# The layers behind attention in an order written by hand: the first stage goes on in cycles, the second runs in two parts of four and five chunks

## The chip, the core and the metric

The kernel runs on one core of a Trainium2 chip. The metric is the device time of one execution in microseconds (us), as the median of several runs. Four engines compute, each with a queue of its own that it works off in order: TensorE (PE, matmuls into PSUM; PEld is its weight load), VectorE (DVE), ScalarE (ACT) and GpSimd (POOL). SyncE (SP) issues the DMAs. [...]

## What is computed

Masked attention over 8 batches, 8 heads, 576 positions and 64 dimensions, and behind it a two-layer network over the 4608 tokens:

```
scores = scale * q @ k^T                 # 8 x 8 x 576 x 576
thresh = max(scores) - tau               # per row
scores = where(scores >= thresh, scores, -1e9)
attn   = softmax(scores);  x = (attn @ v) as 4608 tokens x 512
h = x @ w_in                             # w_in 512 x 2048, float64
g = max(h, 0) + alpha * min(h, 0)        # alpha per column of h
out = g @ w_out                          # w_out 2048 x 512, float64
```

The weights come as float64. Each matrix is used as the sum of a high and a low part in a float32 matmul format, and each product is three matmuls: high x high, low x high and high x low.

## The kernel before

The 2048 hidden columns are 16 chunks of 128. Chunks 0 to 6 (`fcs1`) are the first stage: it runs beside attention, for 18 groups of 256 tokens (`groups1`). Chunks 7 to 15 (`fcs2`) are the second stage, for 9 groups of 512 tokens, behind it. The first stage leaves its sums in DRAM (`part`); the second adds its own and writes `out`.

**One group, one chunk.** The first layer (`layer1_into`, L188 to L201) is 12 matmuls: four slices of the 512 inputs, three products each, with `xh` and `xl`, the parts of x, as the moving operand. Then comes the prelu on DVE, a copy to the high part on ACT and a subtraction for the low part on POOL (`split_g`, L213). The second layer (`layer2`, L220) is three matmuls of 512 columns for each block of 128 tokens and chunk: high part with `woh`, high part with `wol`, low part with `woh`. A group of 256 tokens has two such blocks, a group of 512 has four.

**Decode.** `Split64` (L102) turns a 128 x 512 piece of float64 words into two parts: a DMA of 512 KB (`load`), two ACT passes (`size`, L123 and L124), five or six DVE passes (`clamp` L127, `shift` L130, `sign` L135, `power` L140, `rest` L148 and, on DVE or POOL, L149), an ACT copy (`round`, L144) and a POOL sum (`join`, L152).

**Order.** Everything up to the end of attention stands in a block with an order written by hand for PE, ACT, DVE and POOL (L791): each engine takes its instructions in the order of the text. SP isn't one of these engines. The text is a loop over cycles (L804); a cycle is one of nine steps of a pair of heads, 288 in all (`total`), and `at_cycle(i, fn)` puts a step into cycle i. `Mlp.cycle` (L713) fills each cycle with work of the first stage up to a length of `CYCLE` = 2.6: at most one first-layer chunk (counted as 1.31) and second-layer matmuls (0.216 each). `step_l1` (L664) loads x, splits it one cycle later and holds the next group's chunks back by three cycles (`gap`); a chunk's prelu falls one cycle and its split two cycles after its matmuls, and the group's second layer starts three cycles after its last chunk. `ps_m` has four PSUM buffers for chunks and accumulators alike; in the first stage's pool x, its parts and the block `po` that goes to DRAM have one buffer each.

Behind the loop the order isn't written by hand: a scheduler orders the queues. `Mlp.drain` (L728) does the groups that are left, with four of the second stage's 18 weight pieces after each (`decode_some`, L853; their words have two buffers, tag `w0`), then come the pieces that are left, and then the second stage (L888 to L904): for each group of 512 tokens x in one piece, nine chunks through `hidden` (L868), and four blocks of 27 matmuls each into `accb`, whose result is added on DVE to the sums read back into `pin` (L903) and stored.

In the trace `pha` and `phb` are the first-layer sums of the first and second stage, `acca` and `accb` those of the second layer, `ga` and `gb` the parts behind the prelu, `xr` a piece of x as loaded, `wri`/`wro` the raw words and `wti`/`wto` the working tiles of a piece of `w_in` or `w_out`.

## Time and profile before

| | us |
|---|---|
| median of three runs | 1400.59 (1400.41 to 1401.59) |
| span of the profiled execution | 1397.3 |
| last matmul of attention starts | 830.5 |
| first matmul of the second stage's first group (`phb`) | 941.5 |
| first matmul into `accb` | 969.1 |
| last matmul into `accb` starts | 1393.1 |
| PE busy in 800 to 900 and in 900 to 1000 | 93.3 and 92.0 |
| DVE busy in 800 to 900 and in 900 to 1000 | 74.9 and 67.8 |
| one `xl` split on POOL, 1024 elements a partition | 2.40 (median) |

The span is that of one profiled execution, from its first to its last instruction. "Busy" is the time in which an engine has an instruction under way; matmuls overlap, so the duration of one (0.39 us for 512 columns) is longer than the distance from one to the next. A row of a group of instructions gives the line, the engine, the operation, output <- inputs, the shapes and the count, then busy time and the mean length of one in ns, and the engine's idle time ahead of them with what ended it. A row of the timeline gives start and length in us, and in brackets the idle time before it. A row of the chain of waits gives start and length of one link of the chain that ended last.

### The profile page before, as it was taken

What the parts mean: (1) busy time and instruction counts of PE and PEld (TensorE: products, weight loads), DVE (VectorE), ACT (ScalarE), POOL (GpSimd) and SP (SyncE); (2) the same over time, 40 slices, a digit from 0 to 9 for tenths busy, and PEclk for the clock granted to TensorE, in tenths of its full rate; (3) what the DMA queues carried; (4) which work ended last, traced back from release to release, by engine and by line L of the source; (5) the groups of instructions that cost most, each with busy time, mean ns of one, the idle gap of its engine ahead of it and who ended that gap; (6) DMA issues with size and microseconds to landing.
All of it is one profiled execution on the core that took longest, in us unless ns stands there. A gap on an engine that the chain in (4) does not pass through costs nothing.

```text
span 1397.3 us, 23301 instructions
## 1 busy us (share of the span) xinstructions
PE 1339.4 (96%) x8116; PEld 1181.2 (85%) x8116; DVE 975.7 (70%) x1933; ACT 820.9 (59%) x1843; POOL 762.3 (55%) x821
## 2 busy tenths in 40 slices
PE   5888899999999999999999999888999999999998
PEld 4556789999999999999999998777888888888887
DVE  6999988888888898898888957986323323323332
ACT  7788888888888888888888854453112012111100
POOL 3776676666676666576676557566434124223311
PEclk9999999999999999999999999999999999999999
DMA  8643634545545444454454214433320220111011
GB/s 249 184 127 106 180 105 122 162 116 142 147 117 150 139 134 131 132 154 127 128 160 132 83 57 153 132 109 128 121 74 17 91 91 33 59 61 42 19 61 38
DMA packets 94628, 157.67 MB, mean 113 GB/s; under 512 B 14160, under 2 KB 39024, under 8 KB 94512
## 3 DMA queue, kind: packets, MB, share of 16 engines
q1 hardware_dynamic: 94512, 156.19, 38.4%
q8 instruction: 65, 1.06, 0.3%
q14 instruction: 51, 0.42, 0.1%
HBM read 85.53 MB, written 28.46 MB: 82 GB/s over the span
## 4 chain that ended last, share of the span: by engine, by line
PE 80%; DVE 9%; ACT 4%; DMA 2%; issue 2%; POOL 2%; SPq 0%; DVEq 0%; POOLq 0%; ACTq 0%
PE phb L194 16%; PE accb L224 16%; PE s L395 10%; PE av L542 10%; PE acca L224 9%; PE pha L194 9%; PE t L439 7%; DVE p L430 2%; DVE nmx L410 2%; DMA wri<-in_moe_w_in_dram 1%; PE tk L455 1%; DVE wti L135 1%; POOL wi L152 1%; ACT xb L555 1%; ACT xa L553 1%
## 5 line engine op out<-in xcount | busy, mean ns | idle before, releaser
L410 DVE TENSOR_REDUCE nmx<-s 128x1 f32<-128x576 f32 x288 | 217.0, 753 | 72.6 <-PE s L395 69.5
L215 ACT ACTIVATE gb<-ptb 128x512 fp32r<-128x512 f32 x81 | 50.9, 630 | 337.7 <-DVE ptb L873 337.3
L218 POOL TENSOR_TENSOR gb<-ptb,gb 128x512 fp32r<-128x512 f32 x81 | 104.4, 1290 | 257.0 <-ACT gb L215 256.8
L224 PE MATMUL acca<-wo,ga 128*128 128x512 f32 x756 | 230.7, 419 | 7.2 <-ACT ga L215 4.0
L224 PE MATMUL accb<-wo,gb 128*128 128x512 f32 x972 | 221.9, 389 | 0.0
L224 PEld LDWEIGHTS accb<-wo,gb 128*128 128x128 f32 x972 | 182.4, 188 | 37.9
L430 DVE SCALAR_TENSOR_TENSOR p<-s,thr,p 128x576 f32<-128x576 f32 x256 | 206.6, 807 | 1.3 <-ACT thr L423 0.9
L194 PE MATMUL phb<-xh,wi 128*128 128x512 f32 x648 | 202.9, 392 | 1.1 <-ACT xh L180 1.1
L194 PE MATMUL pha<-xh,wi 128*128 128x256 f32 x1008 | 199.7, 284 | 3.7 <-DVE pta L873 3.4
L418 ACT ACTIVATE p<-s,nmx 128x576 f32<-128x576 f32 x256 | 190.0, 742 | 10.8 <-DVE nmx L410 10.5
L395 PE MATMUL s<-kh,qst 128*128 128x288 f32 x640 | 142.2, 312 | 38.1 <-DVE p L430 23.3
L194 PEld LDWEIGHTS pha<-xh,wi 128*128 128x128 f32 x1008 | 163.8, 190 | 9.9 <-DVE pta L873 4.6
L224 PEld LDWEIGHTS acca<-wo,ga 128*128 128x128 f32 x756 | 132.8, 191 | 28.6 <-ACT ga L215 5.3
L439 PE MATMUL t<-ident,p 128*128 128x128 f32 x1024 | 154.6, 274 | 0.0
L395 PEld LDWEIGHTS s<-kh,qst 128*128 128x128 f32 x640 | 101.4, 193 | 61.5 <-issue 29.4
L903 DVE TENSOR_TENSOR ob<-accb,pin 128x512 f32<-128x512 f32 x36 | 24.2, 689 | 181.9 <-PE accb L224 181.9
L194 PEld LDWEIGHTS phb<-xh,wi 128*128 128x128 f32 x648 | 122.6, 189 | 27.2 <-ACT xh L180 1.5
L194 PE MATMUL pha<-xl,wi 128*128 128x256 f32 x504 | 142.2, 282 | 0.0
L872 DVE TENSOR_SCALAR ptb<-phb,alpha_sb 128x512 f32<-128x512 f32 x81 | 60.7, 751 | 108.5 <-PE phb L194 96.4
L395 PE MATMUL s<-kl,qst 128*128 128x288 f32 x640 | 133.8, 299 | 0.0
L194 PE MATMUL phb<-xl,wi 128*128 128x512 f32 x324 | 127.2, 393 | 3.6 <-POOL xl L182 3.6
L439 PEld LDWEIGHTS t<-ident,p 128*128 128x128 f32 x1024 | 126.5, 141 | 0.1
(117 smaller groups left out, 2772.6 us busy)
## 6 DMA issues: line engine op xcount, KB each, us to landing
kr<-in_k_dram SPq DMA_DIRECT2D x31, 320.0 KB
rb<-rvd SPq DMA_DIRECT2D x64, 144.0 KB
xs<-xa SPq DMA_DIRECT2D x32, 288.0 KB
part<-po SPq DMA_DIRECT2D x36, 256.0 KB
pin<-part SPq DMA_DIRECT2D x36, 256.0 KB
out_dram<-ob SPq DMA_DIRECT2D x36, 256.0 KB
vr<-in_v_dram SPq DMA_DIRECT2D x28, 320.0 KB
qr<-in_q_dram SPq DMA_DIRECT2D x31, 288.0 KB
```

What stands on the lines that cost most here:

```text
L194: nc.tensor.matmul(ph[:, :n], w[:, c, :], xx[:, c, :n], start=(c == 0 and ti == 0), stop=(c == NCC - 1 and ti == 2),)
L215: nc.scalar.activation(g[:, 0, :n], t[:, :n], AF.Copy)
L218: nc.gpsimd.tensor_tensor(g[:, 1, :n], t[:, :n], f(g[:, 0, :n]), op=ALU.subtract)
L224: nc.tensor.matmul(acc[:m, :], gg[:, g, o : o + m], w, start=(first and ti == 0), stop=(last and ti == 2))
L395: nc.tensor.matmul(ps[:, h, :288], w, kk[:, a + h * 288 : a + (h + 1) * 288], start=(ki == 0 and i == 0), stop=(ki == 1 and i == n - 1),)
L410: nc.vector.tensor_reduce(self.nmx[:, j : j + 1], self.S[u][0][:, :, :288], axis=AX.XY, op=ALU.max, negate=True)
L418: nc.scalar.activation(pj, ps[:, :, :288], AF.Exp, bias=nmx[:, j : j + 1], scale=1.0)
L430: nc.vector.scalar_tensor_tensor(pj, ps[:, :, :288], thr[:, j : j + 1], pj, op0=ALU.is_ge, op1=ALU.mult, accum_out=self.sm[:, c : c + 1])
L439: nc.tensor.transpose(tb[:, c, :], pt[:, j, j * D + c * P : j * D + (c + 1) * P], ident)
L542: nc.tensor.matmul(pa[:m, :n], w, x, start=(part == 0 and c == 0), stop=(part == z.parts[-1] and c == NKC))
L872: nc.vector.tensor_scalar(t[:, :n], ph[:, :n], 0.0, alpha_sb[:, fc : fc + 1], op0=ALU.min, op1=ALU.mult)
L903: nc.vector.tensor_tensor(ob[:m], acc[:m], pi_[:m], op=ALU.add)
```

## The change

The written order now holds to the end of the program, and the drain and the scheduler's second stage are gone.

- The cycle loop goes on past `total` until the first stage is empty. There `used` is 0, so a cycle holds 2.6 of the first stage's work alone; a chunk taken at or after `total` (`alone`) has its prelu in two DVE passes (`prelu`) instead of one on DVE, one on ACT and one on POOL, and its high part on ACT.
- At cycle `total + CLOSE` (297) attention's memory is given up. From there the eight pieces of the second stage's first part (chunks 7 to 10) are decoded step by step, one piece every 2.5 cycles (`DEC2` = 5), with three buffers for the raw words, and x of its first group is loaded and split by slices (`fetch_x`, 512 columns a slice, two `xr` buffers).
- The second stage runs in two parts: chunks 7 to 10 over all nine groups of 512 tokens, then chunks 11 to 15 over all nine again. A cycle there is one first-layer chunk or one block of the second layer. Part one adds its sums to those in `part` and stores them there again; part two adds its own and stores to `out`. The ten pieces of part two are decoded under part one, one every six cycles (`DEC3` = 6). x is fetched for the next group in each group, so twice in all.

```diff
-TAIL = 4
+CLOSE = 9
+DEC2, DEC3 = 5, 6
...
+    def prelu(pool, gn, fc, n, ph, name, bufs):
+        t = pool.tile([P, gn], F32, tag="pt", name=f"pt{name}", bufs=bufs)
+        nc.vector.tensor_scalar(t[:, :n], ph[:, :n], 0.0, alpha_sb[:, fc : fc + 1], op0=ALU.min, op1=ALU.mult)
+        nc.vector.scalar_tensor_tensor(t[:, :n], ph[:, :n], 0.0, t[:, :n], op0=ALU.max, op1=ALU.add)
+        return t
...
+            alone = i >= total
+
             def act(ph=ph):
+                if alone:
+                    st[fi] = (prelu(mem.mp1, G1, fcs1[fi], n, ph, name, 2),)
+                    return
                 st[fi] = prelu1(mem.mp1, G1, fcs1[fi], n, ph, name, 2)
                 prelu2(*st[fi], n)
...
+    def decode_at(c, pool, w, fc, io, load):
+        if load is not None:
+            at_cycle(load, w.load)
         at_cycle(c, w.size)
         at_cycle(c + 1, w.clamp)
         at_cycle(c + 2, w.shift)
         at_cycle(c + 3, w.sign)
         at_cycle(c + 4, w.power)
+        at_cycle(c + 4, lambda: w.round(weight(pool, fc, io)[:, 0]))
         at_cycle(c + 5, w.rest)
+        at_cycle(c + 6, lambda: (w.join((wi if io == "i" else wo)[fc][:, 1]), ready.add((io, fc))))
...
+    parts2 = [fcs2[: len(fcs2) // 2], fcs2[len(fcs2) // 2 :]]
+    groups2 = [(t, min(G2, NT - t)) for t in range(0, NT, G2)]
...
+    def decode_part(part, c0, step):
+        for n_, (io, fc) in enumerate((io, fc) for io in "io" for fc in part):
+            w = Split64(mem.wp2, ("w0", 3), mem.wp2, ("w1", 3), ENG2[(fc + (io == "o")) % 2], *(src_i if io == "i" else src_o)(fc))
+            c = c0 + step * n_ // 2
+            decode_at(c, mem.wp2, w, fc, io, c - 2)
+
+    def fetch_x(pool, t0, n, c, name):
...
+        def split(k):
+            if k == 0:
+                st["parts"] = tuple(pool.tile([P, NCC, G2], F32R, tag=t, name=f"{t}{name}", bufs=1) for t in ("xh", "xl"))
+            xr, (xh, xl) = st["xr"][k], st["parts"]
+            nc.scalar.activation(xh[:, k, :n], xr[:, :n], AF.Copy)
+            nc.gpsimd.tensor_tensor(xl[:, k, :n], xr[:, :n], f(xh[:, k, :n]), op=ALU.subtract)
+            if k == NCC - 1:
+                st["x"] = st["parts"]
+
+        for k in range(NCC):
+            at_cycle(c + k, load, k)
+            at_cycle(c + k + 2, split, k)
+        return st
...
-        for i in range(-3, total + TAIL):
+        i = -4
+        first = None
+        while True:
+            i += 1
+            if i > total + CLOSE and not (mlp.l1 or mlp.l2 or nready < len(groups1)):
+                break
...
+            if i == total + CLOSE:
+                at.close()
+                mem.wp2 = wp2_.enter_context(tc.tile_pool(name="wp2", bufs=1, reuse_waits="tile"))
+                decode_part(parts2[0], i + 3, DEC2)
+                first = fetch_x(mem.wp2, *groups2[0], i + 4, "0_0")
...
+            if i >= total:
+                used = 0.0
...
+        todo = [(p, k) for p in range(len(parts2)) for k in range(len(groups2))]
+        nxt = first
+        decode_part(parts2[1], i + 3, 2 * DEC3)
+        for num, (p, k) in enumerate(todo):
+            fcs, (t0, n), st = parts2[p], groups2[k], nxt
+            if num + 1 < len(todo):
+                p_, k_ = todo[num + 1]
+                nxt = fetch_x((mem.wp2, mp2)[(num + 1) % 2], *groups2[k_], i, f"{p_}_{k_}")
...
+            for b, (o, m) in enumerate(blocks):
+                at_cycle(i + len(fcs) - 2 + b, load_pin, o, m)
+            g = []
+            for fc in fcs:
+                ph = ps_2.tile([P, 512], F32, tag="ph", name=f"phb{p}{t0}_{fc}", bufs=4)
+                while "x" not in st:
+                    cycle()
+                layer1_into(ph, fc, n, st["x"])
+                cycle()
+                t = prelu(mp2, G2, fc, n, ph, f"b{p}{t0}_{fc}", 2)
+                gg = mp2.tile([P, 2, G2], F32R, tag="g", name=f"gb{p}{t0}_{fc}", bufs=len(parts2[1]) + 1)
+                split_g(gg, t, n)
+                g.append(gg)
+            for o, m in blocks:
+                acc = ps_2.tile([P, 512], F32, tag="acc", name=f"accb{p}{t0}_{o}", bufs=4)
+                for j, fc in enumerate(fcs):
+                    layer2(acc, fc, g[j], o, m, j == 0, j == len(fcs) - 1)
+                cycle()
+                ob = mp2.tile([P, DM], F32, tag="ob", name=f"ob{p}{t0}_{o}", bufs=3)
+                nc.vector.tensor_tensor(ob[:m], acc[:m], pins[o][:m], op=ALU.add)
+                gi, r = divmod(t0 + o, G1)
+                dst = out[t0 + o : t0 + o + m, :] if p == len(parts2) - 1 else part[gi][r : r + m, :]
+                nc.sync.dma_start(dst, ob[:m])
```

`cycle()` in the last loop runs the steps put into the current cycle and moves on to the next.

## The prediction

> **What bounds the kernel now.** I read the page's head first, then the table of stretches, then what TensorE (PE) waited for, then the rows of the two stages behind attention.

> ```profile
> span 1397.3 us, 23301 instructions
> ...
> 830.50:968.80 138.30, 123.81 (x684) 104.88 (x682) 111.67 (x171) 59.58 (x108) 90.25 (x73) 0.96 0.42 132
> 968.80:1010.00 41.20, 41.20 (x183) 34.12 (x182) 12.16 (x18) 8.44 (x10) 18.41 (x10) 1.00 0.35 117
> 1010.00:1393.50 383.50, 383.50 (x1693) 317.24 (x1691) 121.81 (x171) 55.06 (x76) 118.62 (x77) 1.00 0.16 53
> ```

> The columns of a stretch are its length, then the busy time of PE, weight load, DVE, ACT and POOL, the granted clock, DMA share and GB/s. From 968.8 on PE is busy in every microsecond at clock 1.00; in the 138.3 us between, it is idle for 14.5 us and the mean clock is 0.96. So only that stretch can give anything. How much, I work out from the pace of undisturbed matmuls and their number.

> ```profile
> 830.49 0.27 PE L565 MATMUL rp<-ident,rv 128*9 128x128 f32 x1
> ...
> 836.98 0.28 PE L194 MATMUL pha<-xh,wi 128*128 128x256 f32 x1
> 841.30 9.71 PE L224 MATMUL acca<-wo,ga 128*128 128x512 f32 x42
> 850.84 0.28 PE L194 MATMUL pha<-xh,wi 128*128 128x256 f32 x1
> ...
> 971.71 8.16 PE phb L194 x36
> 979.87 21.99 PE accb L224 x97
> ...
> L224 PE MATMUL acca<-wo,ga 128*128 128x512 f32 x238 | 61.3, 404 | 6.4 <-ACT ga L215 4.0 <-POOL ga L218 2.0
> L194 PE MATMUL pha<-xh,wi 128*128 128x256 f32 x248 | 47.2, 285 | 3.5 <-DVE pta L873 3.4
> L194 PE MATMUL pha<-xl,wi 128*128 128x256 f32 x124 | 35.1, 283 | 0.0
> ...
> L194 PE MATMUL phb<-xl,wi 128*128 128x512 f32 x324 | 127.2, 393 | 3.6 <-POOL xl L182 3.6
> ...
> L224 PE MATMUL accb<-wo,gb x972: 388/389/390, 969.1 to 1393.1; 128*128 128x512 f32 x195
> ...
> L903 DVE TENSOR_TENSOR ob<-accb,pin 128x512 f32<-128x512 f32 x36 | 24.2, 689 | 181.9 <-PE accb L224 181.9
> ```

> Attention's last matmul starts at 830.49. Between 836.98 and 841.30 stand three chunks' first layers, 36 matmuls: 0.120 us each, 1.43 a chunk as they come. 42 second-layer matmuls take 850.84 - 841.30: 0.227 each. 97 accb in 21.99 give the same 0.227, and a 12-matmul chunk of 512 columns 2.72. Left after 830.5 are 238 acca (54.1 us), 248 + 124 pha (44.6), and 3 x 324 phb (a third of them read xl) with 972 accb (1944 x 0.2267 = 440.7): 539.4 us. The last accb starts at 1393.1, so the work took about 562.8, and **23.4 us are lost**. That is the most that the change can win; the same matmuls run after it, at the same pace.

> **What the change puts in place of it.** Decoding of the second part's ten pieces moves under part one, where PE covers it. It costs nothing unless it stands in front of something that PE needs. x is fetched and split twice and the partial sums are read, added and written twice: 36 more DVE adds of 0.69 us and 36 more splits of 512 columns on ACT and POOL, all beside PE; DVE is busy 122 of 383 us today. New waits are the price, in three places.

> *First, the end of a group's first layer.* Today the scheduler runs chunks of the next group in between (the 36 phb at 971.71, before 97 accb), and nine chunks leave 24 matmuls ahead of the last one's need. The new code is inside the hand-ordered block, so PE takes layer two right behind the last chunk. How late are its parts?

> ```profile
> 1050.65 0.39 PE L194 MATMUL phb<-xh,wi 128*128 128x512 f32 x1
> ...
> 1053.64 0.75 DVE L872 TENSOR_SCALAR ptb<-phb,alpha_sb 128x512 f32<-128x512 f32 x1 [2.10 <-PE phb L194]
> 1054.43 0.69 DVE L873 SCALAR_TENSOR_TENSOR ptb<-phb,ptb 128x512 f32<-128x512 f32 x1
> ...
> 1055.24 0.63 ACT L215 ACTIVATE gb<-ptb 128x512 fp32r<-128x512 f32 x1 [26.43 <-DVE ptb L873]
> ...
> 1055.94 1.28 POOL L218 TENSOR_TENSOR gb<-ptb,gb 128x512 fp32r<-128x512 f32 x1 [21.73 <-ACT gb L215]
> ```

> The chunk begun at 1050.65 hands PE on at T = 1050.65 + 2.72 = 1053.37. Its high part is there at 1055.87 (T+2.50) and its low part at 1057.22 (T+3.85, with a hand-over T+3.92). In part one (four chunks) layer two reaches the matmul that needs the low part as its twelfth, at T + 11 x 0.2267 = T+2.49: PE stands for 1.43 us, nine times: **12.9**. In part two (five chunks) it is the fifteenth, T+3.17: 0.75 nine times, **6.8**. No row allows less, since nothing else is in PE's queue there. POOL is the tight engine ahead of it: in the last two chunk cycles it must do one low part (1.28) and one x split of the same 512 columns, some 2.6 of 2.72 us, so whatever else it gets there comes on top. Decode pieces are six cycles apart and a group has eight cycles. Of the ten, the fourth and the eighth place a remainder (L149) and a join (L152) on POOL ahead of that last low part, 1.30 each by the row below, less 0.1 of slack: 2.5, twice: **5.0**.

> ```profile
> 856.02 1.30 POOL L152 TENSOR_TENSOR wo<-wto,wro 128x512 fp32r<-128x512 f32 x1
> ...
> 845.96 0.43 DVE L127 TENSOR_SCALAR wti<-wti 128x512 f32<-128x512 f32 x1 [3.45 <-ACT wti L123]
> ...
> 846.89 0.69 DVE L135 SCALAR_TENSOR_TENSOR wti<-wri,wti 128x512 int32<-128x512 int32 x1
> ...
> 849.71 2.89 DVE L135 SCALAR_TENSOR_TENSOR wto<-wro,wto 128x512 int32<-128x512 int32 x1
> ...
> 849.27 2.78 POOL L182 TENSOR_TENSOR xl<-xr,xh 128x1024 fp32r<-128x1024 f32 x1 [3.54 <-ACT xh L180]
> ```

> The second and third rows are a decode's clamp and sign, undisturbed; the last two bound what I don't count: a sign step, 0.69 alone, was held until POOL's split ended, and the split itself took 2.78 where the median is 2.40. Part one has such steps in most cycles; 0 to 0.5 us a group, 0 to 4.5 in all, for the upper end.

> *Second, the hand-over from one first-stage group to the next.* The loop's rules, walked from cycle 288, give for each of groups 13 to 17: six layer-two matmuls and a chunk four times, three and a chunk, two chunks alone, then the load of x, and 21 layer-two matmuls before the next group's first chunk. xh and xl have one buffer, so nothing is split before the last chunk ends (T): prelu, high part, xh, xl take to T+5.3, and PE is there at T+4.9 (21 x 0.227 and the first matmul): 0.45 at least.

> ```profile
> 841.64 5.87 DMA xr<-xs
> ...
> 868.02 4.42 DMA wri<-in_moe_w_in_dram
> ...
> 868.02 0.38 SPq L113 DMA_DIRECT2D wri<-in_moe_w_in_dram  x1
> ...
> L180 ACT ACTIVATE xh<-xr x27: 1045/1059/1921, 156.0 to 1271.2; 128x1024 fp32r<-128x1024 f32 x18, 128x2048 fp32r<-128x2048 f32 x9
> L182 POOL TENSOR_TENSOR xl<-xr,xh x27: 2373/2402/4708, 157.1 to 1273.2; 128x1024 fp32r<-128x1024 f32 x18, 128x2048 fp32r<-128x2048 f32 x9
> ...
> L872 DVE TENSOR_SCALAR pta<-pha,alpha_sb 128x256 f32<-128x256 f32 x31 | 14.7, 475 | 3.6 <-POOL ga L218 2.6 <-PE pha L194 1.0
> L873 DVE SCALAR_TENSOR_TENSOR pta<-pha,pta 128x256 f32<-128x256 f32 x31 | 12.8, 415 | 0.3
> ...
> L123 ACT ACTIVATE wti<-wri 128x512 f32<-128x512 f32 x9 | 6.0, 671 | 16.0 <-DMA wri<-in_moe_w_in_dram 16.0
> ```

> Groups 14 and 17 have only this. Their load goes out behind the store of the previous block, which three chunks (4.3) precede T; with its copy (0.6), two issues (0.38 each) and hand-overs, some 1.7 by estimate from these rows, that is T-2.6. By the 5.87 row it lands at T+3.3, xl ends 3.5 later, and PE waits 1.8; by 4.5 it is 0.45. I take 1.1, twice: 2.2. Group 15's load stands on SP behind the third load of the part's first x, which waits for a split (two xr buffers); that split ends near T-1.0, so it goes out about T-0.6: -0.6 + 5.87 + 1.06 + 2.40 = T+8.7, so 3.8.

> *Third, the decode of part one's eight pieces*, 2.5 cycles apart with three raw buffers (w0). A piece holds its buffer for eight cycles, from load to join, so the load of piece n+3 waits for the join of piece n, one or two cycles before ACT is to read it. Both of ACT's and DVE's queues are in written order: behind the late size and clamp stand the prelus that free PSUM. With two accumulators, two of ps_m's four buffers are left, and PE runs two chunks and twelve layer-two matmuls, 5.6 us, before it stands. For the fourth piece: split 1.3, join 1.3, load 4.5 (4.42 with a hand-over), size 0.67, clamp 0.43, prelu 0.9 make 9.1, less 5.6: 3.5. For the eighth, without the split, 2.2. The seventh stands ahead of group 16's split: from the join near T, 0.5 + 4.5 + 1.3 + 0.4 + 1.06 + 2.40 = T+10, less 4.9: 5.0. Second and third place together: 2.2 + 3.8 + 3.5 + 2.2 + 5.0 = **16.7**. If SP's loads always run ahead it is 4 x 0.45 = 1.8; these are the two ends, and I take the walk itself because every length in it has a row.

> **Sum.** 12.9 + 6.8 + 5.0 + 16.7 = 41.4 lost against 23.4: **+18.0 us**, a span of 1415.3. The runs' median is 1400.59, 3.3 above the profiled span, so I say **1418.6**.

> **The clock.** The rows tell what a gap costs beyond its length (stretches as above, then PE's rows with the idle time before them):

> ```profile
> 896.00:898.00 2.00, 0.34 (x2) 0.30 (x3) 2.00 (x5) 0.81 (x2) 0.47 (x2) 1.00 0.33 44
> 898.00:900.00 2.00, 2.00 (x8) 1.71 (x7) 1.97 (x4) 1.14 (x3) 2.00 (x2) 0.50 1.00 367
> 900.00:902.00 2.00, 2.00 (x9) 1.68 (x9) 1.93 (x3) 0.16 (x1) 1.26 (x2) 0.65 0.61 185
> ...
> 880.26 0.38 PE L194 MATMUL pha<-xh,wi 128*128 128x256 f32 x1 [1.43 <-DVE pta L873]
> 897.66 1.80 PE L224 MATMUL acca<-wo,ga 128*128 128x512 f32 x4 [2.34 <-ACT ga L215]
> 929.63 0.39 PE L194 MATMUL pha<-xh,wi 128*128 128x256 f32 x1 [2.02 <-DVE pta L873]
> ```

> After the 2.34 gap the granted clock was 0.50, then 0.65: 2 x 0.5 + 2 x 0.35 = 1.7 us lost. After 1.43 and 2.02 it stayed at 1.00. So the boundary waits should not pay this, and up to five gaps of 3.5 to 5 could: +8.5, kept for the upper end. [...]

> **Rivals.**
> *Loads run ahead* (10%). SP is outside the hand-ordered engines, so its loads may go out earlier than in the text. Then the first stage loses 1.8 and POOL's 5.0 shrinks: 12.9 + 6.8 + 1.8 + 0 to 5 = 21.5 to 26.5, 1399 to 1404: no change. For it: the 42 acca at 841.30 ran without a gap while loads landed. Against: three buffers for pieces that need more.
> *Faster* (5%). The boundary waits vanish because something fills them: the last chunk's parts leave DVE, ACT and POOL before layer two arrives, or PE takes the next group's chunk. It decides from 20.6 us of total loss downwards, which needs the 19.7 at the boundaries to go at least in part; without them and with the walk's 16.7 and 5.0 the loss is 21.7, with loads ahead 6.8 at most: 1384 to 1399, about 1390. Against it stand the four latency rows.
> *The clock swings at each boundary* (7%). Should a 1.43 us gap, coming back every 21.7 us, cost as the 2.34 one did, 18 x 1.7 = 31 come on top: 1449.
> *The forecast* (78%): 1405 to 1432, from the walk with half its third place and no POOL delay (41.4 - 5.4 - 5.0 = 31.0 lost, +7.6, 1408), less the 2.2 of the plain hand-overs, to all with clock loss and DVE's holds (18.0 + 8.5 + 4.5 = +31, 1432).

> The range takes the forecast and the upper edge of the first rival, with 2 us left above for an x split that lands late in part two: **1402 to 1434**. A difference under 0.2% (2.8 us) can hardly be told from none. Faster by more: 5%; within: 10%; slower by more: 85%.

> **What will show it.** PE should wait for accb on POOL's gb, 1.4 us nine times and 0.7 nine times, spread evenly over the second stage, where today there is no wait; two of the nine should be near 4. Before it, pha should wait for xl and for pta after ACT's waits for wri and wro; the stretch from attention's end to the first phb should still show gaps. DVE's decode should appear under part one with PE busy. If no accb wait shows, the order of PE isn't the written one, and I am wrong about the direction; if the drain shows no ACT wait on weight words, only about its size.

## The result, and the profile after

The changed kernel takes 1430.9 us (median of four runs, 1429.04 to 1431.76) against 1401.07 for the one before in the same session: a ratio of 1.0216, with a 95% interval of 1.0202 to 1.023. The forecast was 1418.6 with a range of 1402 to 1434. The direction is right and the time lies in the range; the effect is 29.8 us where 18.0 was forecast. The profiled execution is 31.5 us longer (1428.8 against 1397.3).

The stretches behind attention, in the columns explained above (first stage, part one, part two):

```profile
837.90:954.70 116.80, 103.17 (x589) 89.34 (x587) 68.20 (x107) 39.02 (x76) 62.30 (x58) 0.93 0.33 105
954.70:1159.50 204.80, 191.35 (x817) 153.03 (x816) 110.24 (x157) 58.37 (x100) 106.88 (x83) 0.99 0.47 147
1159.50:1425.00 265.50, 259.28 (x1129) 210.59 (x1127) 93.34 (x131) 48.38 (x81) 104.22 (x82) 1.00 0.36 109
```

Before, PE was busy without a break from 968.8 on. Now it has idle time in all three stretches. The table of PE's waits in 837.9 to 1428 names what ended it (us in total, times, longest):

```profile
PE accb L231 <- POOL gb L225: 17.3, 20, 2.8
PE pha L195 <- POOL xl L183: 6.2, 4, 2.1
PE acca L231 <- ACT ga L222: 3.5, 2, 2.6
PE acca L231 <- POOL ga L225: 2.9, 4, 1.1
PE accb L231 <- ACT gb L222: 2.4, 7, 0.3
PE pha L195 <- ACT po L720: 1.0, 1, 1.0
```

The first and the fifth line have no counterpart before. Idle time alone undercounts, because a matmul under a lowered clock is busy too: PE is busy for all of 1044 to 1046 with 6 matmuls at 0.50, and for all of 1118 to 1120 with 11 at 1.00. So for each run I add up, over all matmuls behind attention, by how much the distance from one start to the next exceeds the undisturbed one (0.120 us for 256 columns, 0.227 for 512). I call this the lost time; the first stage is the stretch from attention's last matmul to the first `phb`, the second stage what follows. It gives 23.4 us before, the number that the prediction had from the sums, and 53.3 after: 29.9 more, in accord with the measured 29.8. The remaining 1.6 of the profiled difference lies inside attention: its 321st score matmul already comes at 212.2 in one and 214.0 in the other. That point varies from 210.4 to 214.8 in the profiles of this study, whose kernels share attention's code, so small differences are judged by lost time rather than by the median alone. (Attention's last matmul starts 7.4 us later than before; 5.7 of these are 25 `acca` matmuls that have moved ahead of it, 213 instead of 238 being left behind it.)

| lost us | first stage | second stage | median |
|---|---|---|---|
| before | 16.4 | 7.0, all of it before the steady run from 968.8 | 1401.07 |
| after | 23.7 | 29.6 | 1430.9 |

So the first stage, with fewer weight pieces to decode, loses as much as everything did before, and the second stage's 29.6 is new.

PE's rows in part one, with the idle time in front of them, show how regular it is:

```profile
991.68 0.73 PE L231 MATMUL accb<-wo,gb 128*128 128x512 f32 x2 [0.35 <-ACT gb L222]
993.26 8.68 PE L231 MATMUL accb<-wo,gb 128*128 128x512 f32 x37 [0.85 <-POOL gb L225]
1015.21 0.73 PE L231 MATMUL accb<-wo,gb 128*128 128x512 f32 x2 [0.35 <-ACT gb L222]
1016.81 8.71 PE L231 MATMUL accb<-wo,gb 128*128 128x512 f32 x37 [0.86 <-POOL gb L225]
1038.48 1.03 PE L231 MATMUL accb<-wo,gb 128*128 128x512 f32 x3 [0.27 <-POOL gb L225]
1042.36 10.31 PE L231 MATMUL accb<-wo,gb 128*128 128x512 f32 x37 [2.85 <-POOL gb L225]
```

In each group PE stands first for the last chunk's high part (ACT), runs two matmuls, and stands again for its low part (POOL). From 991.68 to 1015.21 are 23.53 us for 96 matmuls that need 96 x 0.2267 = 21.76: 1.77 lost. The fourth group (1042.36) waits 2.85 instead, and its next 37 matmuls take 10.31 us instead of 8.7.

### The profile page after: what moved, and what is told of

Its sections match the earlier page's. It is cut to its first block, busy times and chain, and to the rows that moved or that the text cites. A ratio compares the mean times of both kernels' runs of the same rounds, so it can differ in the third digit from the quotient of the medians.

```text
span 1428.8 us, 23881 instructions
## 1 busy us (share of the span) xinstructions
PE 1352.3 (95%) x8116; PEld 1184.4 (83%) x8116; DVE 1002.8 (70%) x1970; ACT 844.0 (59%) x1906; POOL 807.3 (57%) x882
## 3 DMA queue, kind: packets, MB, share of 16 engines
q8 instruction: 65, 1.06, 0.3%
## 4 chain that ended last, share of the span: by engine, by line
PE 69%; POOL 11%; DVE 8%; ACT 5%; issue 4%; DMA 2%; SPq 1%; POOLq 0%; ACTq 0%; DVEq 0%
PE accb L231 12%; PE pha L195 11%; PE acca L231 11%; PE av L549 10%; PE s L402 10%; PE t L446 7%; PE phb L195 6%; POOL gb L225 6%; POOL xl L809 3%; DVE p L437 1%; DVE nmx L417 1%; PE tk L462 1%; DVE ptb L213 1%; DVE ptb L214 1%; ACT gb L222 1%
## 5 line engine op out<-in xcount | busy, mean ns | idle before, releaser
L231 PE MATMUL accb<-wo,gb 128*128 128x512 f32 x972 | 233.2, 395 | 19.7 <-POOL gb L225 17.3
L195 PE MATMUL pha<-xh,wi 128*128 128x256 f32 x1008 | 203.6, 286 | 1.2 <-ACT po L720 1.0
L195 PEld LDWEIGHTS pha<-xh,wi 128*128 128x128 f32 x1008 | 166.8, 193 | 6.8 <-ACT po L720 1.6
L936 DVE TENSOR_TENSOR ob<-accb,pin 128x512 f32<-128x512 f32 x72 | 49.8, 692 | 163.8 <-PE accb L231 163.7
L225 POOL TENSOR_TENSOR ga<-pta,ga 128x256 fp32r<-128x256 f32 x126 | 95.9, 762 | 54.7 <-ACT ga L222 47.2
```

The source lines that it names most:

```text
L195: nc.tensor.matmul(ph[:, :n], w[:, c, :], xx[:, c, :n], start=(c == 0 and ti == 0), stop=(c == NCC - 1 and ti == 2),)
L225: nc.gpsimd.tensor_tensor(g[:, 1, :n], t[:, :n], f(g[:, 0, :n]), op=ALU.subtract)
L231: nc.tensor.matmul(acc[:m, :], gg[:, g, o : o + m], w, start=(first and ti == 0), stop=(last and ti == 2))
L936: nc.vector.tensor_tensor(ob[:m], acc[:m], pins[o][:m], op=ALU.add)
```

## The experiments

Two theories of the second stage were set against each other at first. **A**: in the second stage the written order makes PE stand at the end of each group's first layer, longer where POOL has decode steps in front. **B**: the stage is slower for its extra work. For the first stage there were **C** (weight words that come late, in front of prelus and splits on ACT) and **D** (the hand-over from group to group, by the split of x).

### The order of the second stage

**e1**: the loop over the second stage stands outside the hand-ordered block; the same instructions, ordered by the scheduler.

```diff
-        for num, (p, k) in enumerate(todo):        # inside manual_schedule
+    for num, (p, k) in enumerate(todo):            # behind it
```

> The loop of the second stage moved out of the hand-ordered block, so that the scheduler orders its queues; same instructions. Theory A (the written order makes PE wait at the end of each group's first layer: 15.9 us in part one, 7.9 in part two, 5.6 more in the two groups where POOL's decode steps fall in front): the waits of accb for gb go, 24 to 29 us less, 1402 to 1407. Theory B (the second stage is slower for its extra work: x and the sums twice, POOL and DVE in each other's way): less than 5 us gained, 1426 or more.

Measured: 1431.18 us, a ratio of 1.021 to the kernel before in the same session, with its 95% interval [1.0183, 1.0237]. By the total B would have won. The stretches (first and second stage) say something else:

```profile
836.90:984.00 147.10, 115.25 (x589) 95.59 (x587) 112.43 (x162) 56.53 (x106) 86.67 (x73) 0.85 0.34 108
984.00:1425.00 441.00, 440.81 (x1945) 364.67 (x1943) 162.03 (x234) 92.72 (x150) 190.29 (x149) 1.00 0.41 126
```

The second stage loses nothing at all, 440.81 of 441.00, with x fetched twice and the sums read, added and written twice. That work is free there, and B falls; decode, which is gone from this stretch here, stands in the second stage again in e6. But the first stage is 147.1 us long and loses 54.0 instead of 23.7. The scheduler pulled the decode of part two forward: in that stretch the sign step on DVE runs for 18 pieces, against 8 in the changed kernel.

```profile
L136 DVE SCALAR_TENSOR_TENSOR wti<-wri,wti 128x512 int32<-128x512 int32 x9 | 11.0, 1223 | 0.1
...
L136 DVE SCALAR_TENSOR_TENSOR wto<-wro,wto 128x512 int32<-128x512 int32 x9 | 9.0, 998 | 0.1
```

Between 924 and 975, where PE loses most, DVE is busy for 50.6 of 51.0 us, and PE's longest wait there (4.4) is for a prelu on DVE. My expectation missed by 24 us because it took the order of PE alone to change. What the run does show is that the written order keeps the first stage 30 us shorter and pays with boundary waits. That the decode pulled forward makes these 30 us is read from DVE's rows; no run holds only the decode back.

**e2**: the order stays written by hand, but one chunk of the next group stands ahead of this group's second layer, with x fetched half a group earlier.

```diff
+            while len(gs.get(num, [])) < len(fcs):
+                chunk(num)
+            fetch(num + 2)
+            if num + 1 < len(todo):
+                chunk(num + 1)
             for o, m in blocks:
```

> Still in written order, but one first-layer chunk of the next group stands ahead of the second layer of this one, and x is fetched half a group earlier for it; instructions and their number are the same. A: 2.72 us of cover against waits of 1.4 and 0.75 us, so 23.8 us less, and the two late groups (3.0 us more) lose at most 1 us each: 1401 to 1408. B: within 4 us of 1431. Last group keeps its 0.87.

Measured: 1409.87 us, 1.0057 [1.0036, 1.0079], 2 us over the expectation's upper end. The second stage loses 9.0 instead of 29.6. All but 0.87 of it, in the last group, lies between 960 and 980: the first group's successor had no x yet. From there to the last group nothing is lost, the two late groups included. The rows of the waits name it:

```profile
PE phb L195 <- POOL xl L809: 3.2, 3, 1.8
...
PE accb L231 <- POOL gb L225: 0.5, 1, 0.5
```

**e3**: part two's last sums (`rest`, `join`) on DVE instead of POOL.

```diff
+            if part is parts2[1]:
+                w.eng, w.add = [nc.vector] * 3, nc.vector
```

> The last three sums of part two's ten decode pieces run on DVE instead of POOL. A: the fourth and the seventh group of part one lose 1.8 us like the others instead of 5.4 and 3.8, so 5.6 us less, about 1425. Rival: the steps on DVE are held while POOL runs, the prelus come late behind them, and several groups lose 0.5 to 1.5 us more: 1429 to 1440.

Measured: 1424.43 us, 1.0169 [1.0142, 1.0196]. The fourth and the seventh group of part one lose 2.0 and 1.9 instead of 5.4 and 3.8, and the second stage 25.0 instead of 29.6, 4.6 less where 5.6 was expected. (In the profile attention's end came at 834.5 and not at 837.9, so not all of the median's 6.5 is this.) The rival is refuted: the other groups stay near 1.8.

**e6**: e2 and e3 together, with the chunk ahead from the second group on only.

```diff
-            if num + 1 < len(todo):
+            if 0 < num < len(todo) - 1:
                 chunk(num + 1)
```

> One chunk ahead as before, but from the second group on (the first group's x of the next one wasn't there: 8.2 us lost), and part two's last sums on DVE. If the second stage's whole excess is order and POOL's queue, it loses 1.8 in the first group, 0.9 in the last and under 2 between, against 29.6; the first stage keeps its 23 to 25, about the 23.4 that was lost before the change: 1402 to 1407. If DVE's decode steps now come late in front of prelus, 1408 or more.

Measured: 1403.39 us, 1.0021 [1.0009, 1.0034]. The second stage loses 2.6 (1.8 in the first group, 0.9 in the last), the first stage 23.6:

```profile
838.00:954.70 116.70, 103.00 (x589) 89.41 (x587) 68.22 (x107) 39.04 (x76) 62.14 (x58) 0.93 0.33 105
954.70:1398.00 443.30, 441.54 (x1945) 364.40 (x1943) 213.64 (x303) 108.01 (x180) 197.08 (x149) 1.00 0.42 133
```

With that the second stage is settled: order and POOL's queue made 27 of its 29.6, and the decode under part one costs PE nothing there.

**e10**: the parts swapped in size, five chunks first and four after.

```diff
-    parts2 = [fcs2[: len(fcs2) // 2], fcs2[len(fcs2) // 2 :]]
+    parts2 = [fcs2[:5], fcs2[5:]]
```

> The parts of the changed kernel swapped in size: part one five chunks (and ten pieces to decode in the first stage), part two four. If a boundary's wait is set by the number of chunks alone, part one loses 0.87 a group and part two 1.77, so 7.9 and 15.9, the sum as before; POOL's late groups are two again, now the third and the fifth of part one, 2 to 3.6 us more each; the first stage's two more pieces cost 0 to 4: 1430 to 1436. If part one's larger wait came from its decode, part one stays at 1.5 or more a group and part two at 0.9 or less.

Measured: 1435.28 us, 1.025 [1.0231, 1.0269]. The second stage loses 29.4, like before the swap. Part two, now of four chunks, loses 1.5 a group, and part one 1.1 to 1.3 while pieces are decoded and 0.9 in its last three groups; the late groups are the third and the fifth (3.1 and 4.7). So the number of chunks sets most of the wait, and decode in the same group adds 0.2 to 0.4: four chunks cost 1.5 without it and 1.77 with it, five 0.87 and about 1.2. Both sides of the expectation were too plain. The two additional pieces cost the first stage 7.2 (30.9 lost), more than the 0 to 4 that I gave them.

### The first stage

**e4**: the eight pieces of part one start three cycles apart instead of 2.5, so that a raw buffer is free before its next load is due.

```diff
-DEC2, DEC3 = 5, 6
+DEC2, DEC3 = 6, 6
```

> DEC2 6 instead of 5: part one's eight pieces start three cycles apart instead of 2.5, so a raw buffer is free before the load that takes it is due. Theory C (late loads in front of prelu and split on ACT make the waits at groups 15 to 17): ACT's 16 us of waiting for wro shrink below 6, the 2.9 us gap at group 16 goes with its clock loss, 4 to 7 us less, 1424 to 1427. Rival D (the waits come from the split of x and of the last chunk, whatever the decode does): within 2 us of 1431.

Measured: 1428.08 us, 1.0196 [1.0166, 1.0227]. ACT's waits for `wro` fall from 16.1 us (four, the first line) to 0.8 (one, the second):

```profile
ACT wto L124 <- DMA wro<-in_moe_w_out_dram: 16.1, 4, 8.8
ACT wto L124 <- DMA wro<-in_moe_w_out_dram: 0.8, 1, 0.8
```

One wait of 7.5 for a `wri` appears, the gap of 2.6 us for `ga` at group 16 is gone, and the first stage loses 20.4 instead of 23.7. C holds, with a smaller price than expected. The waits for xl stay, 7.9 us against 6.2. The second stage loses 33.3, 3.7 more: its two late groups wait as before (2.84 each, against 2.85 and 2.84), but the clock falls after both, and they lose over 6 each, against 5.4 and 3.8 in the changed kernel.

**e5**: from attention's end on, x is split in four slices.

```diff
+        for c in range(NCC):
+            nc.scalar.activation(xh[:, c, :n], xr[:, c, :n], AF.Copy)
+            nc.gpsimd.tensor_tensor(xl[:, c, :n], xr[:, c, :n], f(xh[:, c, :n]), op=ALU.subtract)
```

> From attention's end on, x of a first-stage group is split in four slices of 256 columns (ACT, POOL, ACT, POOL ...) instead of one pass of 1024 on each; all else as in the changed kernel. Theory D (the next group's first chunk waits for the whole xl, 7.0 us in four hand-overs, and the half clock behind comes from those gaps): those four waits fall below 0.5 us each and some of the clock loss goes, 6 to 12 us less, 1419 to 1425. Rival C (late weight words on ACT set them): within 2 us of 1431.

Measured: 1430.1 us, 1.0217 [1.02, 1.0234]. The waits for xl fall from 6.2 to 0.5 us, as D said, and yet the first stage loses 22.7 instead of 23.7; the 6 to 12 us that D promised don't come. The waits moved to the next in line:

```profile
PE acca L239 <- ACT ga L230: 3.5, 2, 2.6
PE pha L203 <- ACT po L729: 3.3, 2, 1.7
PE acca L239 <- POOL ga L233: 2.7, 3, 1.1
...
PE pha L203 <- POOL xl L191: 0.5, 1, 0.5
```

**e7**: the second stage's first x is fetched and split behind the decode, 27 cycles later.

```diff
-                first = fetch_x(mem.wp2, *groups2[0], i + 4, "0_0")
+                first = fetch_x(mem.wp2, *groups2[0], i + 31, "0_0")
```

> The second stage's first x is fetched and split in cycles 328 to 333 instead of 301 to 306, behind the decode of part one. The prediction's second place says that these loads and splits make the hand-over to group 15 late (3.8 of its waits): that hand-over falls from 7 us with clock loss to 3 to 5, 2 to 4 us less in the whole, 1427 to 1429. Rival: DVE's decode steps, held while POOL splits, make it late by themselves: within 1.5 us there.

Measured: 1430.51 us, 1.0217 [1.0192, 1.0241]. The first stage loses 21.6, 2.1 less; in 870 to 880, where group 15 is handed over, 3.9 instead of 5.9. In the total nothing shows: the second stage lost 32.6 in this profile, because the clock fell behind both late groups, as in e4, at 1.6 us or more each.

**e9 and e8**: e6 with spacing and slices (e9), and with the late fetch as well (e8).

> The kernel with all edits but the late first x of the second stage: it comes in cycles 301 to 306 again. Alone, spacing the pieces took 3.3 us off the first stage's loss, slices 1.0, the late fetch 2.1; together 11.1. If each removes what hid behind the other, the fetch costs more here than its 2.1 alone: first stage 15 to 18 lost against 12.5, 1393 to 1397. If spacing and slices do it between them: within 1.5 us of 1390.8.

> All of it together: a chunk ahead, part two's sums on DVE, pieces three cycles apart, x of the first stage in slices, the second stage's first x late. If the places add: second stage 3 to 5 lost, first stage 8 to 14, so 11 to 19 against 23.4 before the change: 1389 to 1397, the fastest. If the first stage's gaps only move to the next queue (DVE's decode behind POOL), it keeps 20 and the kernel is level with the one before, 1401 to 1405.

Measured: e9 1394.42 us, 0.9964 [0.9954, 0.9974]; e8 1390.79 us, 0.9941 [0.9922, 0.996], faster than the kernel before. The first stage loses 14.3 in e9 and 12.5 in e8, the second 2.6 in both. The places don't add: spacing and slices took 3.3 and 1.0 us off alone and 9.3 together. Split up, the part of the loss that stands at PE's gaps does add: it fell by 3.8 and 1.5 alone and by 5.2 together. The clock doesn't. In the first stage it stands at one half for 17.1 us in the changed kernel, in e4 and in e5 alike, and for 3.4 in e9; the mean of the stretch is 0.93, 0.92, 0.93 and 0.98. The late fetch is worth 1.8 there, near its 2.1 alone, less than e9's expectation had it. The stretches of e8 and its waits of PE:

```profile
835.90:941.40 105.50, 100.98 (x588) 87.13 (x586) 62.73 (x107) 40.31 (x88) 66.78 (x70) 0.97 0.37 116
941.40:1388.70 447.30, 441.76 (x1945) 364.55 (x1943) 213.88 (x304) 107.84 (x180) 197.05 (x149) 1.00 0.42 133
```

```profile
PE accb L240 <- POOL gb L234: 1.5, 2, 0.9
PE acca L240 <- POOL ga L234: 1.5, 3, 0.8
PE pha L204 <- POOL xl L192: 1.3, 4, 0.5
PE acca L240 <- ACT ga L231: 1.1, 1, 1.1
```

Each ratio is to the kernel before in the same session (medians 1399.43 to 1401.68), and each lost time is that of one profile. Whether a gap brings the clock down varies from profile to profile and is worth 1.6 us or more, so that differences of 1 to 2 us in one column (e5's 1.0, e7's 2.1) are not clear of chance.

| lost us | first stage | second stage | median, ratio |
|---|---|---|---|
| changed kernel | 23.7 | 29.6 | 1430.9, 1.0216 |
| e1 scheduler's order | 54.0 | 0.0 | 1431.18, 1.021 |
| e2 a chunk ahead | 25.1 | 9.0 | 1409.87, 1.0057 |
| e3 sums on DVE | 24.6 | 25.0 | 1424.43, 1.0169 |
| e6 e2 and e3 | 23.6 | 2.6 | 1403.39, 1.0021 |
| e10 parts swapped | 30.9 | 29.4 | 1435.28, 1.025 |
| e4 spaced pieces | 20.4 | 33.3 | 1428.08, 1.0196 |
| e5 slices of x | 22.7 | 30.1 | 1430.1, 1.0217 |
| e7 late first x | 21.6 | 32.6 | 1430.51, 1.0217 |
| e9 e6, e4, e5 | 14.3 | 2.6 | 1394.42, 0.9964 |
| e8 e9 and e7 | 12.5 | 2.6 | 1390.79, 0.9941 |

## Why the prediction was right, and where its sizes were off

**What bounds the kernel.** The 23.4 us were right to the tenth when summed matmul by matmul in the trace. That no more than these could be gained is contradicted by no run: the best one, e8, still loses 15.1, and is 8.3 of them faster than before by its ratio.

**The boundaries.** The mechanism is shown (e2 and e6 take it away, e10 moves it). Part one was put at 12.9 and is 15.8 without its two late groups' extra, part two at 6.8 and is 8.1. The walk ended when the low part was there. PE then lost some 0.1 more per stop before it was at its pace again (0.11 behind each of the stops at 1015.21 and 1016.81), and while pieces were being decoded a group lost 0.2 to 0.4 us more (e10), which I had kept for the upper end as 0 to 4.5.

**POOL's two late groups.** Predicted for the fourth and the eighth piece, 2.5 each. They stand in the fourth and the seventh group, which lost 3.6 and 2.0 us more than the others; 1.6 of the 3.6 is a lowered clock. POOL's queue in the fourth group shows the remainder (L150) and the join (L153) ahead of the last low part at 1041.04:

```profile
1034.62 1.29 POOL L150 TENSOR_TENSOR wti<-wti,wi 128x512 f32<-128x512 f32 x1
...
1037.12 1.30 POOL L225 TENSOR_TENSOR gb<-ptb,gb 128x512 fp32r<-128x512 f32 x1
1038.37 1.49 POOL L153 TENSOR_TENSOR wi<-wti,wri 128x512 fp32r<-128x512 f32 x1
1039.82 1.26 POOL L809 TENSOR_TENSOR xl<-xr,xh 128x512 fp32r<-128x512 f32 x1
1041.04 1.26 POOL L225 TENSOR_TENSOR gb<-ptb,gb 128x512 fp32r<-128x512 f32 x1
```

e3, which takes these two steps off POOL, shows the cause. The total, 5.6 against 5.0, is near by luck: the wait alone was 2.0 a group, and the clock made up the rest.

**The first stage.** 16.7 were forecast and 23.7 are lost: the sum is mis-sized by 7.0, the largest error, and its parts lie elsewhere. Lost by hand-over: 4.9 us at group 14, 7.2 at 15, 8.8 at 16, 1.4 at 17, and 1.3 at 914.7, where PE waits for ACT's copy of a block to `po`. The distances that hold a gap make 15.8 of the 23.7; that this is near the forecast's 16.7 is luck, since terms that were too large and too small cancel.

At group 14 I had 1.1. What I left out are attention's own last steps, which stand on POOL among the last chunks' low parts and ahead of xl (read from the rows; no run moves them):

```profile
844.53 1.21 POOL L596 TENSOR_TENSOR xa<-xa,rb 128x576 f32<-128x576 f32 x1 [1.91 <-DMA rb<-rvd]
845.69 0.73 POOL L225 TENSOR_TENSOR ga<-pta,ga 128x256 fp32r<-128x256 f32 x1
846.82 1.21 POOL L602 TENSOR_TENSOR xa<-xa,rb 128x576 f32<-128x576 f32 x1 [0.40 <-DVE rb L599]
847.99 0.72 POOL L225 TENSOR_TENSOR ga<-pta,ga 128x256 fp32r<-128x256 f32 x1
848.67 2.35 POOL L183 TENSOR_TENSOR xl<-xr,xh 128x1024 fp32r<-128x1024 f32 x1
```

At group 15 I had the load of x behind another on SP (3.8). That did not happen: the load went out at 853.44, behind the split of group 14 and 19 us ahead of its own, and those of groups 16 and 17 went out as early (876.65 and 906.33). The early first x of the second stage costs time here all the same, by way of POOL and DVE. Its splits on POOL (866.25, 868.82 and 871.46) stand among the last chunks' low parts, and DVE's decode steps, 0.42 us alone, take up to 1.5 beside them, with the last chunks' prelus behind:

```profile
866.75 1.51 DVE L128 TENSOR_SCALAR wti<-wti 128x512 f32<-128x512 f32 x1
...
869.04 1.37 DVE L141 TENSOR_SCALAR wri<-wti 128x512 int32<-128x512 int32 x1
870.32 0.96 DVE L131 TENSOR_SCALAR wti<-wti 128x512 int32<-128x512 int32 x1
871.21 0.47 DVE L213 TENSOR_SCALAR pta<-pha,alpha_sb 128x256 f32<-128x256 f32 x1
```

In e7, without these splits, the three steps take 0.96, 0.42 and 0.42, PE's waits for the last chunk's parts (0.93 and 0.49) are gone, and the place loses 2.0 less; the wait for xl itself, 2.1 us, stays. Which of POOL and DVE does it was not separated.

For the fourth piece I had PE standing 3.5 for PSUM. ACT did wait 4.9 us for its words (to 883.24), but no row of PE stands there. The other traces say why: a lowered clock hid it. Behind group 15's gap the clock is at one half until 882.75, and PE comes to the place late itself. In e2, e3, e5 and e7 the clock was back more than 2.5 us before the words came, and there PE does wait for the copy to `po` behind them: 0.62, 1.06, 1.58 and 1.30 us. In e1, e6 and e10, as in the changed kernel, it came back within half a microsecond of the words, and PE doesn't wait. For the seventh piece, 5.0: group 16's hand-over is that place, its gaps cost 6.4, and e4 shows that late words make the longest of them, 2.6 us for `ga`. For the eighth, 2.2: 1.3, since ACT's copy to `po` stands behind its words, which ACT took up at 912.99. I had expected waits for the prelu (`pta`); none shows.

The clock is the rest: 7.9 of the 23.7 are matmuls at a lower rate. I had seen this cost, counted at most 8.5 for it, and left it out of the sum, although three of the waits that I had forecast there (3.5, 3.8 and 5.0; the prediction says five, its own sum has three) were longer than the 2.34 that had lowered the clock before. That was the step that was mis-sized: a cost that the rows showed stood only in the range.

**The rivals.** *Loads run ahead* came true for x, as said, but not for the weight words, on which its price hung: the load of the fourth piece went out at 878.35, behind the join that ended then. *Faster* did not happen, since the written order is kept. *The clock swings at each boundary*: of eighteen, one group shows it (below). Behind the waits of 0.35 and 0.85 us that return every 23.5 us the clock stayed at 1.00 in the changed kernel.

## What to carry to other kernels

When a hand-written order replaces a scheduler's, walk one group from its last matmul to the first that needs its result, engine by engine: what the matmuls in between don't cover is paid in each group, and one chunk of the next group put in between removed all of it here, in every group that had one. Smaller groups of work multiply such boundaries, so splitting nine chunks into four and five is only free with that chunk ahead. Where a stage has several causes of waiting, taking one away can show little (1.0 and 3.3 us) and taking two away more than the sum (9.3): the gaps added up here, but the clock came near full rate (0.98, against 0.92 and 0.93 with one of them) only when both causes were gone. And a total that doesn't move, as in e1, can hide 30 us won in one stage and lost in the other.

## What the runs showed of the hardware

The same gap lowered the clock once and once not. The fourth and the seventh group of part one wait 2.85 and 2.84 us behind the same short run of matmuls. After the first the granted clock was 0.79 and 0.50, after the second 1.00:

```profile
1042.00:1044.00 2.00, 1.65 (x6) 1.32 (x7) 1.03 (x2) 0.00 (x0) 1.54 (x2) 0.79 0.70 220
1044.00:1046.00 2.00, 2.00 (x6) 1.61 (x5) 0.00 (x0) 0.63 (x1) 0.64 (x1) 0.50 0.65 218
1116.00:1118.00 2.00, 1.41 (x6) 1.19 (x7) 0.87 (x2) 0.00 (x0) 1.78 (x2) 1.00 0.53 139
1118.00:1120.00 2.00, 2.00 (x11) 1.64 (x10) 0.28 (x2) 0.63 (x1) 1.22 (x1) 1.00 0.47 134
```

```profile
1039.77:1043.18 3.41, 0.82 (x4) 0.69 (x5) 0.29 (x1) 0.63 (x1) 3.41 (x4) 1.00 0.57 175
1043.18:1046.59 3.41, 3.41 (x10) 2.63 (x9) 0.74 (x2) 0.63 (x1) 1.59 (x2) 0.50 0.69 195
1111.45:1114.86 3.41, 2.05 (x8) 0.98 (x6) 1.46 (x3) 1.71 (x3) 3.41 (x3) 1.00 0.28 77
1114.86:1118.27 3.41, 1.68 (x7) 1.41 (x8) 1.02 (x2) 0.20 (x1) 2.92 (x3) 1.00 0.31 82
```

The first lies almost whole in one step, in which PE is idle for 2.59 of 3.41 us (76%), and the next step runs at 0.50. The second is cut in two, idle for 40 and 51%, and the clock stays at 1.00. In this trace, behind attention, the clock fell after steps with 54, 60, 76 and 76% idle. The share alone doesn't settle it: the step from 875.92, itself at 0.50, was idle for 22%, and the next one ran at 0.50 again. What share is enough was not shown. In the first stage two gaps of 1.02 and 1.69 us with half a microsecond of matmuls between them were enough for 0.51 and 0.64:

```profile
852.00:854.00 2.00, 2.00 (x9) 1.81 (x8) 0.83 (x2) 0.00 (x0) 0.00 (x0) 0.51 0.97 275
854.00:856.00 2.00, 2.00 (x9) 1.61 (x9) 0.08 (x1) 1.66 (x3) 0.74 (x1) 0.64 1.02 345
```

So a single gap's cost can't be given as one number. The late groups' gaps of 2.84 to 2.92 us in the changed kernel, e4, e5 and e7 cost nothing beyond their length twice, 1.6 to 1.9 us three times, when one step ran at half clock, and 2.5 to 2.6 three times, when two did.

What stays open: which of POOL and DVE makes the hand-over to group 15 late, whether DVE's decode alone makes the 30 us of e1's first stage, and what makes attention's first 210 us differ by some 4 us between profiles of kernels whose attention is the same.
